# Projection tiles in four matmuls of 512 columns: tables and stores turned to that token order

## The chip, the cores and the metric

The kernel runs on one NeuronCore of a Trainium2 chip: TensorE (PE, with its weight loads shown apart as PEld), VectorE (DVE), ScalarE (ACT), GpSimd (POOL), a queue engine (SyncE, SP), and 16 DMA engines between HBM and the on-chip memory. Results of TensorE land in PSUM, eight banks of 512 float32 columns on 128 partitions. The metric is the device time of one execution in microseconds; smaller is better. Engines run their own instructions in the order in which they were issued and meet only at semaphores.

## What is computed

Attention with an exponential feature map over 8 batches, 8 heads, 576 tokens and 64 features a head; its output, 512 features a token, goes through a gated long convolution:

```python
proj = np.einsum('bhsd,df->bhsf', x, w_phi)            # phi(x), for q and for k
proj = proj - np.max(np.abs(proj), axis=-1, keepdims=True)
phi  = np.concatenate([np.exp(proj), np.exp(-proj)], axis=-1)
kv, z = einsum('bhsf,bhsd->bhfd', k_p, v), np.sum(k_p, axis=2)
x = (q_p @ kv) / (q_p . z + 1e-06)                     # then 512 features a token
x1, x2, x3 = np.split(x @ w_proj, 3, axis=-1)          # w_proj is 512 x 1536
x2_conv = np.fft.irfft(np.fft.rfft(x2, axis=1) * np.fft.rfft(filter_fft, axis=0), n=576, axis=1)
out = (x1 * x2_conv * x3) @ w_out                      # 8 x 576 x 512, float32
```

The Fourier transforms are matmuls with tables of sines that the kernel makes for itself at its start.

## The kernel before

**Tokens.** A token is 9 t + j, with t from 0 to 63 and j from 0 to 8. The 64 tokens of j = 4 go a way of their own (the steps whose names end in `t`). The other 512 stand in four blocks of 128, numbered a = 2 g + d: g is the lower or upper half of the t, d = 0 holds j = 0 to 3, and d = 1 holds j = 8 to 5, kept mirrored (t and j both falling), since the transform works on sums and differences of a token and its mirror image.

**Order of work.** A planner's word list, `PLAN` (L31 to L197), fixes the order: each word is one step with its batch, its part and its PSUM bank (`X1,3,2@4`), the steps are issued in the order of the list, and each engine and each queue works its own steps in that order. Batches overlap: the attention of one batch stands between the convolution steps of the batches before it. The steps that matter here:

- `Pq` and `ex` (L658, L686) make the feature tiles `Eq` of the queries; `NE` (L772) picks a block of `Eq` for each a and multiplies it with `KVs`; `xn` (L795) divides and writes 128 tokens by four blocks by 128 features of a pair of heads.
- `trx` (L816) turns `xn` of one pair of heads, v = 0 to 3, into `xT` by a DMA transpose on SP's queue. `trh` (L602) does the same for q and k of a later batch, `trxt` (L821) for j = 4.
- `f1`, `f2` (L845, L851) form sums and differences of the blocks of `xn`, `F` (L856) multiplies them with the table `D`, and `X2` (L893), `Y1`, `m3` and `I` (L967) carry the convolution on to the inverse table `inv`, whose columns are tokens in the order that `gi_nr` (L337) lays down.
- `X1` and `X3` call `proj` (L914): one tile is 128 output features by the 512 tokens, summed over the four kt (the v of `xT`). Each batch has four tiles of `X1` and four of `X3`, 64 tiles in all. It fills one PSUM bank with eight matmuls of 256 columns: first d = 0 for the four kt, then d = 1 for the four kt, reading the d = 1 blocks backwards, so that its tokens come out rising. Each matmul loads its 128 by 128 weights first.
- `O` (L1017) multiplies with `wout`, `Oe` (L1023) copies 128 tokens by 512 features to one of four `o` buffers, and `st` (L1026) sends each half of it, 64 rows of 2 KB, to rows j, j + 9, j + 18, ... of the output. Nine halves go out for each batch: two for each c of 0 to 3, and one for c = 4, the tokens of j = 4 of a pair of batches. c = 0 and 1 hold j = 0 to 3, c = 2 and 3 hold j = 5 to 8. 67 of the 72 stores are issued on SP's queue, and five of the last batch on ACT's.

SP's queue carries the transposes and the stores in one order. An `o` buffer is written again only when both its stores have landed.

Of the kernel before, what the change touches and what calls it, by code (L numbers as in the profile page):

```python
# [16 lines left out]
SEQ = 576  # L17
# [4 lines left out]
IOTA = dict(allow_small_or_imprecise_dtypes=True)  # L22
# [20 lines left out]
mlo,DVE,0 maxkt,0@2 trm,0@6 rve,DVE,1@0 em,m,0,0 em,m,0,1 trme,DVE,0@6 em,p,0,0 vs,POOL,m,0,0  # L43
trh,k,1,1 Pqt,0@4 exkt,p,0@2 Qn,1,0@6 Pq,0,1@0 exqt,p,0@4 maxq,1,0@6 exqt,m,0@4 fl_loadt em,p,0,1
ex,q,m,0,1@0 Qn,1,3@6 vs,DVE,p,0,0 load,k,2 Pq,0,2@4 Pq,0,3@2 ex,q,p,0,1@0 w_load,proj,2
maxq,1,3@6 vs,POOL,p,0,1 ex,q,p,0,3@2 Pk,1,1@0 maxk,1,1@0 KV,0,0@6 ex,q,m,0,3@2 ex,q,p,0,2@4
Qnt,1@2 w_load,proj,0 KVe,DVE,0,0@6 ex,q,m,0,2@4 vs,POOL,m,0,1 maxqt,1@2 NE,0,1@6 Qn,1,2@2
ex,k,p,1,1@0 rc,0,1@6 Pq,0,0@4 xn,0,1@6 ft,ACT maxq,1,2@2 trx,0,1 KV,0,1@6 load,v,1 ex,k,m,1,1@0
load,q,2 trh,k,2,0 ex,q,p,0,0@4 Pk,1,0@0 KVe,DVE,0,1@6 w_load,proj,1 maxk,1,0@0 NE,0,2@6
ex,q,m,0,0@4 zl,POOL NE,0,3@2 rc,0,2@6 Pk,1,3@4 ex,k,p,1,0@0 xn,0,2@6 rc,0,3@2 NE,0,0@6  # L50
ex,k,m,1,0@0 xn,0,3@2 rc,0,0@6 NEt,0@2 f1,POOL,0,1,1 ex,k,p,1,3@4 xn,0,0@6 Pkt,1@0 rct,0@2
# [4 lines left out]
X1,0,3@1 late He,ACT,2,0@7 maxk,1,2@4 f2,POOL,0,0,0 He,ACT,3,1@2 X1,0,2@6 He,ACT,1,1@0 mlo,DVE,1  # L56
X1,0,0@7 X1e,DVE,0,3@1 f2,POOL,0,0,1 ex,k,m,1,2@4 He,DVE,3,0@2 trm,1@3 X1e,ACT,0,0@7 trh,q,2,0
vs,DVE,m,1,0 F,0,3@4 load,v,2 trme,ACT,1@3 F,0,1@0 Fe,ACT,0,3@4 X3,0,0@2 X1e,DVE,0,2@6 em,m,1,1
vs,POOL,p,1,0 trh,k,2,1 Fe,ACT,0,1@0 F,0,2@4 tm,0,0@2 F,0,0@6 Fe,ACT,0,2@4 Pq,1,1@0 Fe,ACT,0,0@6
Pk,2,0@2 vs,POOL,m,1,1 KV,1,0@4 ex,q,p,1,1@0 maxk,2,0@2 ex,q,m,1,1@0 X2,0,3@7 KVe,DVE,1,0@4  # L60
em,p,1,1 ex,k,p,2,0@2 X3,0,2@6 vs,POOL,p,1,1 Y1,0,3@7 Xl,ACT,0 X2,0,2@1 trxt,0 ex,k,m,2,0@2
# [10 lines left out]
exqt,p,1@2 ym,POOL,0,3 trx,1,3 xn,1,2@0 NEt,1@2 KVe,ACT,2,0@4 O,0,3@6 rct,1@2 f2,DVE,1,0,0 trx,1,2  # L72
f2,DVE,1,0,1 O,0,0@7 f1,DVE,1,1,1 Oe,ACT,0,3@6 f1,DVE,1,1,0 xnt,1,1@2 Qn,2,3@4 f2,POOL,1,1,1
Qnt,2@0 xnt,1,0@2 O,0,1@6 maxq,2,3@4 O,0,2@3 Oe,ACT,0,1@6 Oe,DVE,0,0@7 F,1,0@4 f2,DVE,1,1,0
Oe,ACT,0,2@3 st,SP,0,0,1 F,1,1@6 maxqt,2@0 Fe,ACT,1,0@4 trh,q,3,1 F,1,3@2 Fe,DVE,1,1@6 F,1,2@0
Fe,ACT,1,3@2 Qn,2,2@4 Fe,ACT,1,2@0 trx,1,0 Pk,2,3@6 maxq,2,2@4 X2,1,1@3 ex,k,m,2,3@6 X2,1,2@0
trh,q,3,0 ex,k,p,2,3@6 Y1,1,1@3 X2,1,3@1 mhi,2 maxk,2,3@6 mlo,POOL,2 trh,k,4,1 load,q,4 trm,2@5
X1,1,3@2 trme,ACT,2@5 load,v,3 Y1,1,2@0 X1,1,2@4 st,SP,0,2,0 X1e,ACT,1,3@2 st,SP,0,3,1 Pq,2,1@2
Y1,1,3@1 X1e,ACT,1,2@4 Qn,3,2@6 em,m,2,1 X1,1,0@4 ex,q,p,2,1@2 maxq,3,2@6 m3,POOL,1,1 X3,1,2@5
ex,q,m,2,1@2 Pq,2,0@0 X1e,ACT,1,0@4 tm,1,2@5 Qn,3,0@6 em,p,2,1 ex,q,p,2,0@0 X3,1,0@3 vs,POOL,m,2,1  # L80
maxq,3,0@6 ex,q,m,2,0@0 NE,2,1@4 tm,1,0@3 Pq,2,2@6 Xl,ACT,1 rc,2,1@4 Pkt,3@0 X3,1,3@2 xn,2,1@4
vs,POOL,p,2,1 exkt,p,3@0 exkt,m,3@0 trx,2,1 NE,2,0@4 ex,q,p,2,2@6 tm,1,3@2 X2,1,0@3 rc,2,0@4
xn,2,0@4 trxt,1 ex,q,m,2,2@6 X1,1,1@2 Y1,1,0@3 f1,POOL,2,0,0 Pqt,2@6 trh,k,4,0 X1e,ACT,1,1@2
KV,2,1@4 maxkt,3@0 exqt,m,2@6 exqt,p,2@6 f1,DVE,2,0,1 Pk,3,1@2 st,SP,0,2,1 KVe,ACT,2,1@4 Pq,2,3@0
f2,POOL,2,0,1 maxk,3,1@2 trx,2,0 NE,2,2@6 ex,q,p,2,3@0 X2,1,4@4 m3,POOL,1,0 rc,2,2@6 ex,q,m,2,3@0
xn,2,2@6 trh,q,4,1 X1t,1@5 Y1,1,4@4 NEt,2@6 X1te,ACT,1@5 NE,2,3@0 ex,k,p,3,1@2 trx,2,2 rct,2@6
# [113 lines left out]
class Kernel:  # L200
# [136 lines left out]
    def gi_nr(self):  # L337
        g, s = self.nc.gpsimd, self.scr
        self.nr = s.tile([128, 288], FP32, name="nr")
        g.iota(self.nr[:, 0:256], pattern=[[5, 2], [1, 4], [9, 32]], base=1,  # L340
               channel_multiplier=0, **IOTA)
        g.iota(self.nr[:, 256:288], pattern=[[9, 32]], base=5, channel_multiplier=0, **IOTA)

    def ident(self):
# [409 lines left out]
    def KV(self, b, X):  # L754
        for w in range(2):
            v = 2 * X + w
            for s, g in enumerate("pm"):
                E, Ft = self.at("Ek" + g, 4 * b + v), self.at("Fk" + g, b)
                vg = self.turn_of("v" + g, (b, X))
                a = (2 * w + s) * 65  # L760
                for j in range(9):
                    for u in range(2):
                        r = slice(64 * u, 64 * u + 64)
                        e = E[r, j % 2, j // 2, :] if j < 8 else Ft[r, w, X, :]
                        self.mm(self.pb(u, a, a + 65), e, vg[r, w, j, :], start=(j == 0),  # L765
# [6 lines left out]
    def NE(self, b, v):  # L772
        KVs = self.at("KVs", b)
        for u in range(2):
            for a in range(4):
                for s, g in enumerate("pm"):
                    y = 2 * (1 - u if a % 2 else u) + a // 2
                    E = self.turn_of("Eq" + g, (b, v))[:, y, a % 2, :]
                    self.mm(self.pb(u, 65 * a, 65 * a + 65), E, KVs[:, u, v, s, :],  # L779
                            start=(s == 0), stop=(s == 1))  # L780

    def NEt(self, b):
        KVs = self.at("KVs", b)
        for X in range(2):
            for u in range(2):
                for s, g in enumerate("pm"):
                    E = self.at("Fq" + g, b)[:, 2 * X + u].rearrange("f w t -> f (w t)")
                    self.mm(self.pb(X, 130 * u, 130 * u + 130), E,
                            KVs[:, u, 2 * X:2 * X + 2, s, :], start=(s == 0), stop=(s == 1))
# [66 lines left out]
    def F(self, b, v):  # L856
        xf, xt, D, Dt = self.at("xf", b), self.at("xnt", b), self.at("D"), self.at("Dt")
        for e in range(2):
            self.mm(self.pb(e, 0, 288), xt[:, v // 2, :], Dt[:, v % 2, 288 * e:288 * e + 288],  # L859
                    start=True, stop=False)  # L860
        for e in range(2):
            for s in range(2):
                self.mm(self.pb(e, 144 * s, 144 * s + 144), xf[:, v, 2 * s + e, :],  # L863
                        D[:, 288 * e + 144 * s:288 * e + 144 * s + 144], start=False,
                        stop=(s == 1))

    def Ft(self, b, X, bank2):
        xt, Dt = self.at("xnt", b), self.at("Dt")
        for e in range(2):
            for w in range(2):  # L870
                r, bank = slice(64 * w, 64 * w + 64), bank2 if w else self.bank
                self.mm(self.ps[:, bank + e, 0:288], xt[r, X, :],
                        Dt[r, w, 288 * e:288 * e + 288], start=True, stop=False)

    def Fs(self, b, v):
        xf, D = self.at("xf", b), self.at("D")
        for e in range(2):
            for s in range(2):
                self.mm(self.pb(e, 144 * s, 144 * s + 144), xf[:, v, 2 * s + e, :],
                        D[:, 288 * e + 144 * s:288 * e + 144 * s + 144], start=False,  # L880
                        stop=(s == 1))

# [30 lines left out]

    def proj(self, b, f0, m):  # L914
        w, x = self.at("wproj"), self.at("xT", b)
        o = self.pb(0).rearrange("p (g d x) -> p d g x", g=2, d=2)
        for d in range(2):
            for kt in range(4):
                y = x[:, kt].rearrange("p (g d) x -> p d g x", g=2)
                self.mm(o[:, d], w[:, kt, f0 + 128 * m:f0 + 128 * m + 128],  # L920
                        y[:, 1, ::-1, ::-1] if d else y[:, 0], start=(kt == 0),
                        stop=(kt == 3))

    def projt(self, b, f0):
        w, x = self.at("wproj"), self.at("xTt", b)
# [47 lines left out]
                self.mm(self.pb(e, 0, 288), l, inv[:, 2 * e + i if i < 2 else 4 + e, :],  # L973
                        start=(i == 0), stop=(i == 2))

    def It(self, b, m):
        c, inv = slice(128 * m, 128 * m + 128), self.at("inv")
        for e in range(2):
            r = slice(64 * e, 64 * e + 64)
            self.mm(self.pb(e, 0, 288), self.at("T4", b)[r, c], inv[r, 4 + e, :], start=True,  # L980
                    stop=False)

    def Is(self, b, m):
        c, inv = slice(128 * m, 128 * m + 128), self.at("inv")
        for e in range(2):
            for i in range(2):
                self.mm(self.pb(e, 0, 288), self.at(f"T{2 * e}", b)[:, i, c],
                        inv[:, 2 * e + i, :], start=False, stop=(i == 1))

    def Ie(self, b, m):  # L990
        self.nc.scalar.copy(self.turn_of("es", (b, m)), self.pb(0, 0, 288))  # L991

# [32 lines left out]

    def st(self, eng, b, c, i):  # L1026
        o = self.turn_of("o", (b, c))
        bb, j = (b, (0, 2, 5, 7)[c] + i) if c < 4 else (b - 1 + i, 4)
        dict(SP=self.nc.sync, ACT=self.nc.scalar)[eng].dma_start(
            out=self.out[bb][j:SEQ:9, :], in_=o[64 * i:64 * i + 64, :])  # L1030

    def run(self):
        self.scratch = ExitStack()
# [52 lines left out]
```

## Time and profile before

| | us |
|---|---|
| median of three runs | 308.5 (307.57 to 310.66) |
| the profiled execution | 307.3 |
| its span, first to last instruction | 305.5 |

A row of a group reads: line, engine, operation, tiles out and in, shape, count, then busy time and mean time of one, then the idle time of the engine just before such instructions and what ended it. In the chain of work that ended last, each piece has its start, its length and its engine. Matmuls are pipelined: the duration of one is longer than the distance to the next, so their pace is read from a run of them in the chain. The issue of a DMA is a row of the queue's engine (SPq, ACTq); its time to landing runs from there to its last completion.

| engine | busy us | share of the span |
|---|---|---|
| TensorE | 275.5 | 90% |
| VectorE | 262.3 | 86% |
| ScalarE | 223.0 | 73% |
| GpSimd | 216.4 | 71% |

### The profile page before, as it was taken

The numbers are of one execution on the slowest core, as the hardware profiler recorded it, in microseconds if no ns is written. First come the engines' busy times: TensorE is split into PE (matmuls) and PEld (weight loads), VectorE is DVE, ScalarE is ACT, GpSimd is POOL, SyncE is SP. The second block draws the span as 40 slices with busy tenths as digits, with TensorE's granted clock in tenths as the row PEclk, the third lists the DMA queues.
The fourth block names the chain that finished last, engine by engine and source line by source line (L and its number), as shares of the span: only waits on it lengthen the run. The fifth ranks groups of instructions, "written<-read, shape, count | busy, mean of one in ns | idle before, by whom it ended". The sixth has DMA issues, their size and how long they took to land.

```text
span 305.5 us, 10146 instructions
## 1 busy us (share of the span) xinstructions
PE 275.5 (90%) x4253; PEld 199.7 (65%) x4287; DVE 262.3 (86%) x448; ACT 223.0 (73%) x360; POOL 216.4 (71%) x180
## 2 busy tenths in 40 slices
PE   8357687999989999999999999999999889999993
PEld 3235654778558876767767776777577656786751
DVE  7798799898897998799988999787997899789863
ACT  1998986888359978876987688976757988843240
POOL 8346968699528689869799998956289397970240
PEclk9855999999999999999999999999999999999998
DMA  7997999999989987997699959994063440322056
GB/s 144 242 200 133 206 136 179 157 153 191 108 118 187 144 136 134 189 177 144 131 151 154 140 92 177 165 163 102 4 139 65 103 89 10 72 55 60 2 120 190
DMA packets 72734, 40.18 MB, mean 132 GB/s; under 512 B 53040, under 2 KB 67504, under 8 KB 72688
## 3 DMA queue, kind: packets, MB, share of 16 engines
q1 hardware_dynamic: 57472, 22.62, 45.4%
q0 software_dynamic: 14816, 16.25, 35.6%
q8 instruction: 33, 0.54, 0.8%
q10 hardware_dynamic: 400, 0.66, 0.6%
q14 instruction: 13, 0.11, 0.1%
HBM read 33.75 MB, written 9.44 MB: 141 GB/s over the span
## 4 chain that ended last, share of the span: by engine, by line
PE 69%; DVE 15%; ACT 5%; DMA 5%; issue 4%; SPq 0%; DVEq 0%
PE ps L920 15%; PE ps L898 9%; PE ps L1020 8%; PE ps L973 6%; PE ps L765 5%; DMA xT<-xn 5%; PE ps L779 3%; DVE mk L708 3%; PE ps L666 3%; PE ps L929 2%; PE ps L672 2%; PE ps L639 2%; PE ps L859 2%; PE ps L318 2%; PE ps L863 2%
## 5 line engine op out<-in xcount | busy, mean ns | idle before, releaser
L920 PE MATMUL ps<-xT,wproj 128*128 128x256 bf16 x512 | 64.2, 273 | 2.3 <-DMA xT<-xn 2.2
L920 PEld LDWEIGHTS <-wproj 128*128 128x128 bf16 x512 | 48.3, 98 | 12.7 <-issue 2.9
L708 DVE TENSOR_REDUCE mk<-ps 128x8 f32<-128x1024 f32 (+1 forms) x40 | 44.2, 1109 | 6.1 <-PE ps L632 5.4
L708 DVE TENSOR_REDUCE mq<-ps 128x8 f32<-128x1024 f32 (+1 forms) x40 | 44.0, 1109 | 5.1 <-PE ps L639 3.6
L912 POOL TENSOR_TENSOR T<-T,T 128x1024 bf16<-128x1024 bf16 x15 | 31.9, 2127 | 18.3 <-DVE T L908 18.2
L1009 POOL TENSOR_TENSOR yT<-cv,x1s 128x576 bf16<-128x576 f32 x27 | 34.3, 1295 | 11.6 <-DVE cv L994 11.5
L750 POOL TENSOR_TENSOR vm<-vn,vm 128x1152 bf16<-128x1152 bf16 x15 | 32.9, 2194 | 9.3 <-ACT vm L744 9.3
L694 ACT ACTIVATE Ekp<-ps 128x1024 bf16<-128x1024 f32 x32 | 33.1, 1033 | 3.9 <-PE ps L632 2.6
L694 ACT ACTIVATE Ekm<-ps 128x1024 bf16<-128x1024 f32 x32 | 33.0, 1032 | 4.0 <-DVE mk L708 2.6
L750 POOL TENSOR_TENSOR vp<-vn,vp 128x1152 bf16<-128x1152 bf16 x15 | 32.2, 2155 | 5.1 <-ACT vp L744 5.1
L694 ACT ACTIVATE Eqp<-ps 128x1024 bf16<-128x1024 f32 x32 | 32.8, 1026 | 3.4 <-PE ps L672 3.2
L1020 PE MATMUL ps<-wout,yT 128*128 128x512 bf16 x130 | 34.0, 380 | 1.2 <-DVE yT L1009 0.4
L694 ACT ACTIVATE Eqm<-ps 128x1024 bf16<-128x1024 f32 x32 | 32.5, 1028 | 3.3 <-PE ps L672 2.5
L847 POOL TENSOR_TENSOR SD<-xn 128x512 bf16<-128x512 bf16 x23 | 26.3, 1160 | 10.1 <-DVE xn L798 8.6
L853 POOL TENSOR_TENSOR xf<-SD 128x512 bf16<-128x512 bf16 x24 | 27.8, 1169 | 7.1 <-DVE SD L847 5.7
L898 PE MATMUL ps<-wproj,XF 128*128 128x512 bf16 x116 | 30.3, 380 | 0.9 <-ACT XF L299 0.2
L973 PE MATMUL ps<-inv,T 128*128 128x288 bf16 x192 | 27.6, 286 | 0.1
L994 DVE TENSOR_TENSOR cv<-es,ps 128x288 f32<-128x288 f32 x64 | 25.6, 443 | 1.4 <-ACT es L991 1.1
L299 ACT CAST x1s<-ps 128x512 bf16<-128x512 f32 (+1 forms) x34 | 17.9, 543 | 11.8 <-PE ps L920 9.9
L961 DVE TENSOR_TENSOR x1s<-ps,x1s 128x512 bf16<-128x512 f32 x32 | 21.7, 684 | 5.0 <-PE ps L920 4.1
L991 ACT COPY es<-ps 128x288 f32<-128x288 f32 x32 | 12.9, 404 | 14.2 <-PE ps L973 13.7
L798 DVE TENSOR_TENSOR xn<-ps,r 128x512 bf16<-128x512 f32 x32 | 22.0, 689 | 0.9
(176 smaller groups left out, 657.5 us busy)
## 6 DMA issues: line engine op xcount, KB each, us to landing
out_dram<-o SPq DMA_DIRECT2D x67, 128.0 KB, 2.5
vn<-in_v_dram POOLq DMA_DIRECT2D x8, 576.0 KB, 7.2
qn<-in_q_dram POOLq DMA_DIRECT2D x7, 576.0 KB, 9.2
kn<-in_k_dram POOLq DMA_DIRECT2D x7, 576.0 KB, 9.2
wproj<-in_moe_w_proj_dram POOLq DMA_DIRECT2D x3, 512.0 KB, 8.5
fl<-in_moe_filter_fft_dram SPq DMA_DIRECT2D x8, 128.0 KB, 5.6
out_dram<-o ACTq DMA_DIRECT2D x5, 128.0 KB, 3.0
qn<-in_q_dram POOLq DMA_DIRECT2D x2, 288.0 KB, 6.5
```

The source lines that it names most:

```text
L694: self.nc.scalar.activation(e, p, AF.Exp, bias=0.0, scale=1.0 if g == "p" else -1.0)
L708: self.nc.vector.tensor_reduce(out=out, in_=src, axis=AX.X, op=ALU.max, apply_absolute_value=True)
L750: self.eng(eng).tensor_tensor(out=t[:, :, :, 0:64], in0=self.at("vn", b)[:, 2 * X:2 * X + 2], in1=t[:, :, :, 64:65].to_broadcast([128, 2, ...
L847: self.eng(eng).tensor_tensor(out=o[:, :, 2 * i:2 * i + 2, :], in0=x[:, :, 0:2, :], in1=x[:, :, 2:4, :], op=ALU.subtract if i else ALU.add)
L853: self.eng(eng).tensor_tensor(out=o[:, :, 2 * i:2 * i + 2, :], in0=x[:, :, 0:4:2, :], in1=x[:, :, 1:4:2, :], op=ALU.subtract if i else ALU ...
L898: self.mm(self.pb(0), l, w[:, kt, 512:1024], start=(kt == 0), stop=(kt == 3))
L912: self.eng(eng).tensor_tensor(out=Y, in0=Y, in1=self.at(f"T{2 * e + 1}", b), op=ALU.add)
L920: self.mm(o[:, d], w[:, kt, f0 + 128 * m:f0 + 128 * m + 128], y[:, 1, ::-1, ::-1] if d else y[:, 0], start=(kt == 0), stop=(kt == 3))
L973: self.mm(self.pb(e, 0, 288), l, inv[:, 2 * e + i if i < 2 else 4 + e, :], start=(i == 0), stop=(i == 2))
L994: self.nc.vector.tensor_tensor(out=self.turn_of("cv", (b, m))[:, :, odd, :], in0=self.turn_of("es", (b, m)).rearrange("p (x t) -> p x t", ...
L1009: self.eng(eng).tensor_tensor(out=self.at("yT", b)[:, m, 0:SEQ], in0=self.turn_of("cv", (b, m)).rearrange("p x h t -> p (x h t)"), in1=sel ...
L1020: self.mm(self.pb(0), y[:, kt, 128 * c:128 * c + 128], w[:, kt, :], start=(kt == 0), stop=(kt == 3))
```

## The change

`proj` issues four matmuls of 512 columns, one for each kt, and reads each `xT[:, kt]` straight through. The mirrored blocks are no longer read backwards, so they keep their falling order up to the output. `NE` picks the blocks of `Eq` for d = 1 in the order that fits, `F` takes the differences of d = 1 in that order, `gi_nr` writes the token numbers of the mirrored half falling (two iota of 128 columns in place of one of 256), and the stores of c = 2 and 3 (32 of the 72) go to rows whose t falls: their destination, 64 rows with one step between them before, becomes two halves h of 32 rows t each, with t walked backwards. `PLAN` is the same word for word, and so is the number of stores and of bytes. Four functions that no step called (`Ft`, `Fs`, `It`, `Is`) are taken out.

```diff
@@ gi_nr
-        g.iota(self.nr[:, 0:256], pattern=[[5, 2], [1, 4], [9, 32]], base=1,
-               channel_multiplier=0, **IOTA)
+        for d in range(2):
+            z = 1 - 2 * d
+            g.iota(self.nr[:, 128 * d:128 * d + 128], pattern=[[z, 4], [9 * z, 32]],
+                   base=288 if d else 1, channel_multiplier=0, **IOTA)
         g.iota(self.nr[:, 256:288], pattern=[[9, 32]], base=5, channel_multiplier=0, **IOTA)
@@ NE
-                for s, g in enumerate("pm"):
-                    y = 2 * (1 - u if a % 2 else u) + a // 2
-                    E = self.turn_of("Eq" + g, (b, v))[:, y, a % 2, :]
+                for s, sg in enumerate("pm"):
+                    g, d = a // 2, a % 2
+                    y = 2 * (1 - u) + 1 - g if d else 2 * u + g
+                    E = self.turn_of("Eq" + sg, (b, v))[:, y, d, :]
@@ F
-                self.mm(self.pb(e, 144 * s, 144 * s + 144), xf[:, v, 2 * s + e, :],
+                self.mm(self.pb(e, 144 * s, 144 * s + 144), xf[:, v, 2 * (1 - s) + 1 if e else 2 * s, :],
@@ proj
-        o = self.pb(0).rearrange("p (g d x) -> p d g x", g=2, d=2)
-        for d in range(2):
-            for kt in range(4):
-                y = x[:, kt].rearrange("p (g d) x -> p d g x", g=2)
-                self.mm(o[:, d], w[:, kt, f0 + 128 * m:f0 + 128 * m + 128],
-                        y[:, 1, ::-1, ::-1] if d else y[:, 0], start=(kt == 0),
-                        stop=(kt == 3))
+        for kt in range(4):
+            self.mm(self.pb(0), w[:, kt, f0 + 128 * m:f0 + 128 * m + 128],
+                    x[:, kt].rearrange("p a x -> p (a x)"), start=(kt == 0), stop=(kt == 3))
@@ st
-        bb, j = (b, (0, 2, 5, 7)[c] + i) if c < 4 else (b - 1 + i, 4)
+        bb, j = (b, (0, 2, 8, 6)[c] + (-i if c > 1 else i)) if c < 4 else (b - 1 + i, 4)
+        dst = self.out[bb][j:SEQ:9, :]
+        if c in (2, 3):
+            dst = dst.rearrange("(h t) d -> h t d", h=2)[:, ::-1, :]
         dict(SP=self.nc.sync, ACT=self.nc.scalar)[eng].dma_start(
-            out=self.out[bb][j:SEQ:9, :], in_=o[64 * i:64 * i + 64, :])
+            out=dst, in_=o[64 * i:64 * i + 64, :])
```

More of the change, by code (lines that the diff above doesn't have):

```diff
@@ L862, in F @@
             for s in range(2):
-                self.mm(self.pb(e, 144 * s, 144 * s + 144), xf[:, v, 2 * s + e, :],
[L864 to L879, printed above, removed]
+                self.mm(self.pb(e, 144 * s, 144 * s + 144), xf[:, v, 2 * (1 - s) + 1 if e else 2 * s, :],
                         D[:, 288 * e + 144 * s:288 * e + 144 * s + 144], start=False,
@@ L974, in I @@
                         start=(i == 0), stop=(i == 2))
[L976 to L988, printed above, removed]
     def Ie(self, b, m):
```

## The prediction

> **What bounds the kernel now.** The page comes first: the span, the busy shares, the chain that ended last, then the groups of the changed matmuls and the issues of the stores.
>
> ```profile
> span 305.5 us, 10146 instructions
> ...
> PE 275.5 (90%) x4253; PEld 199.7 (65%) x4287; DVE 262.3 (86%) x448; ACT 223.0 (73%) x360; POOL 216.4 (71%) x180
> ...
> q1 hardware_dynamic: 57472, 22.62, 45.4%
> ...
> q10 hardware_dynamic: 400, 0.66, 0.6%
> ...
> PE 69%; DVE 15%; ACT 5%; DMA 5%; issue 4%; SPq 0%; DVEq 0%
> ...
> L920 PE MATMUL ps<-xT,wproj 128*128 128x256 bf16 x512 | 64.2, 273 | 2.3 <-DMA xT<-xn 2.2
> L920 PEld LDWEIGHTS <-wproj 128*128 128x128 bf16 x512 | 48.3, 98 | 12.7 <-issue 2.9
> ...
> out_dram<-o SPq DMA_DIRECT2D x67, 128.0 KB, 2.5
> ```
>
> TensorE bounds the kernel: 90% busy, 69% of the chain. The DMA pieces of the chain are 5%, all of them `xT`: transposes that arrive as PE wants them. The changed matmuls are 64.2 us of busy time, so the question is first how much quicker a tile becomes. That is read from the chain in order of time (start, length, what):
>
> ```profile
> 141.25 4.13 DMA xT<-xn
> ...
> 272.91 0.58 SPq L1029
> 273.54 2.51 DMA xT<-xn
> ...
> 283.42 0.86 PE ps L898 x4
> 284.28 0.86 PE ps L1020 x4
> 285.14 2.62 PE ps L920 x24
> ```
>
> Three projection tiles back to back take 2.62 us, so 0.873 for a tile of eight; four matmuls of 512 columns, as `X2` and `O` have them, take 0.86. The matmul goes by its columns, and the 98 ns of a weight load hide behind 109 ns of matmul already. One reads here that halving the number of matmuls halves neither time nor anything on the path.
>
> **The change part by part.**
>
> *The tiles.* 64 tiles gain about 0.01 us each: 0.64 us. A second gain is at late transposes. PE's timeline:
>
> ```profile
> 144.25 0.50 PE L920 MATMUL ps<-xT,wproj 128*128 128x256 bf16 x3
> 145.42 1.58 PE L920 MATMUL ps<-xT,wproj 128*128 128x256 bf16 x13 [0.67 <-DMA xT<-xn]
> ...
> 275.73 1.29 PE L920 MATMUL ps<-xT,wproj 128*128 128x256 bf16 x8
> ```
>
> At 144.25 the tile stops after three matmuls, because kt = 3 is not there; five of 0.109 are still to do when it lands (0.55), after the change one of 0.215: 0.33 less. The tile at 275.73, which waits for kt = 1, has seven left (0.76), then three (0.65): 0.11 less. With one more stop like the first that makes about 0.8. Together -1.4 us; the ends are 0 (if all of it is eaten by waits of other engines) and -1.4. A rule says more: the Trainium skill, "TensorE: Matmul & The Clock Gate", section "Back-to-back issue gap", gives about 131 ns for each matmul of 512 columns in a sustained stream, which would make a tile 0.52 us and the gain 64 x 0.35 = 22 us. The rows above show 215 ns, which is the isolated formula of the same section (512 / 2.4 + 2.5), so I don't count with 131.
>
> *`NE`, `F`.* The same number of matmuls and loads of the same shapes, other indices: nothing to either side. *`PLAN`*: no step passes another.
>
> *`gi_nr`.* One iota of 256 columns becomes two of 128, at the start on POOL, ahead of two q and k loads on POOL's queue.
>
> ```profile
> 3.72 0.42 POOL L340 IOTA nr<- 128x256 f32 x1
> 4.06 0.19 POOL L342 IOTA nr<- 128x32 f32 x1
> ...
> 4.66 2.06 DVE L422 TENSOR_SCALAR turn<-nr,cols 128x288 f32<-128x288 f32 x5
> ```
>
> An iota of 128 lies between 0.19 (32 columns) and 0.42 (256), so the pair costs between -0.04 and 0.42 more; about 0.2. DVE reads `nr` at 4.66, 0.4 after it is done at 4.25, which covers it, and without that cover it would be 0.2. I count 0.
>
> *The stores of c = 2 and 3.* This part decides. The destination was 64 rows with one step; now it is two halves of 32 rows, with 2 as its outermost count. How is a store spread over the 16 DMA engines? The DMA view of 0 to 14 us and of 291 to 306 us (queue, packets, MB, share of 16 engines):
>
> ```profile
> q1 hardware_dynamic: 800, 1.11, 25.5%
> ...
> fl<-in_moe_filter_fft_dram SPq DMA_DIRECT2D x8, 128.0 KB, 5.6
> ...
> phi<-in_w_phi_dram SPq DMA_DIRECT2D x2, 32.0 KB, 4.3
> ```
>
> ```profile
> GB/s 0 0 0 98 224 186 197 235 131 38 218 208 208 197 180 0 60 202 224 197 104 191 322 175 246 339 290 251 355 208 322 284 224 186 16 0 0 0 0 0
> ...
> q1 hardware_dynamic: 1040, 1.70, 49.6%
> q10 hardware_dynamic: 400, 0.66, 12.1%
> ...
> out_dram<-o SPq DMA_DIRECT2D x13, 128.0 KB, 2.4
> out_dram<-o ACTq DMA_DIRECT2D x5, 128.0 KB, 3.0
> ```
>
> Five ACT stores make 400 packets, 80 each: 64 rows and 16 more, one completion for each engine. The 13 on SP do the same (1040 / 13), and the ten early loads too (800 / 10), though `fl` walks 32 by 2 rows: its outermost count is 32. So each transfer here has an outermost count that 16 divides, and goes to 16 engines in equal parts. No row shows a count of 2. The bounds are: still 16 engines (no cost), or whole outer slices to an engine, which is two engines with 32 rows each. I take two, as what is seen fits a split of the outer count and nothing in it would split an inner one. The Trainium skill says so outright: "DMA: Bandwidth & Descriptors", section "Why a DMA increments its semaphore by 16 and not by 1", has a transfer run on the largest k up to 16 that divides both sides' slowest counts, and for queues like SP's and ACT's on the lowest-numbered k. The 16 completions agree; k = 2 is in no run yet.
>
> The price of a row: q10 kept the engines busy for 12.1% of 16 x 15 us, 29 us for 320 rows, 91 ns. q1 gives 119 us for 832 rows, 143 ns, its waits included. The best slice, 355 GB/s, is 22.2 GB/s an engine, 92 ns for 2 KB. I take 92, as two of the three agree, and 143 as the upper end. A store then holds two engines for 32 rows, 2.94 us, where it held all 16 for 4 rows, 0.37: +2.58, and what stands behind it on SP's queue waits that long on those two engines; I take a transpose to use all 16, as a store does now, so that it lands late as a whole. (By the same DMA page, section "Specifications", 27 GiB/s an engine would make a row 71 ns, and the end of the kernel, next, about 6 us shorter.)
>
> *The end.* Of the 18 stores issued from 291.21 on, eight are turned (batches 6 and 7, c = 2 and 3).
>
> ```profile
> 291.21 10.43 SPq L1029 DMA_DIRECT2D out_dram<-o  x13
> ...
> DMA to landing us min/median/max: 2.2/2.6/10.5
> ```
>
> The two engines get 8 x 32 + 10 x 4 = 296 rows, 27.2 us. The first byte moves at about 293.0 (issue, plus the least landing of 2.2, less 0.37 of its own rows), so the last lands at 320.2, where now it is about 304.2 (301.2 for the last issue and 3.0 on ACT): +16.0. The engines don't run dry: batch 7's copies wait for `o` buffers, but batch 6's stores alone are 13 us of rows. The tiles' gain moves the start of this stretch, so it stays in the sum.
>
> *Before the end.* 24 more turned stores. The lower bound is 0, all hidden; the upper 24 x 2.58 = 62 us, each on the path. I count the three places where rows show little room.
> - `trx,7,1` at 273.54 lies in the chain right behind a turned store (272.91): +2.6.
> - `trh,q,7,1`: two transposes of q of batch 7 follow four stores, three of them turned.
>
> ```profile
> 222.77 2.39 SPq L1029 DMA_DIRECT2D out_dram<-o  x4
> 225.28 2.76 SPq L603 DMA_TRANSPOSE qT<-qn  x2
> ...
> DMA to landing us min/median/max: 3.3/3.3/3.3
> ...
> 230.88 0.40 PE L639 MATMUL ps<-wphi,qT 64*128 64x128 bf16 x8
> ```
>
> The first lands at 225.28 + 3.3 = 228.6, and `Qn` reads it at 230.88, 2.3 later. Three times 2.58 is 7.7, so PE stops for 5.4. Less if the queue is late in issuing anyway.
> - `trx,3,3` at 141.25, in the chain, two us behind a turned store:
>
> ```profile
> 139.28 0.55 SPq L1029 DMA_DIRECT2D out_dram<-o  x1
> 139.92 2.55 SPq L817 DMA_TRANSPOSE xT<-xn  x2
> ```
>
> +2.6, and 7.7 if the two turned stores ten us before it are still in the way. Everywhere else I count 0: what hides it is the time between a transpose's landing and its use, and 2.58 a store is the cost if that is gone.
>
> Sum: -1.4 + 16.0 + 2.6 + 5.4 + 2.6 = +25.2 on the profiled execution's 307.3 (span 305.5 and 1.8 around it), 332.5 us. That execution is 1.2 under the median of 308.5, so the change is given against either as some 8%.
>
> **The rivals.**
> - *The stores keep 16 engines* (the other side): the queue folds the two halves into 64 rows, or splits the inner count. For it: no transfer of before used fewer. Against: a falling step inside a rising one can't be one step, and nothing seen splits an inner count. Then only the tiles count: 307.3 - 1.4 = 305.9, within 1%. It decides with 16 completions to a store.
> - *Two engines, but only the end pays*: the middle has room, since DMA is 5% of the chain. Against: that 5% is just such transposes. 307.3 - 1.4 + 16.0 = 321.9.
> - *The middle pays more*: rows at 143 ns beside the loads, `o` buffers that come free late and hold up ScalarE: each 2.58 beyond the three counted, from `trx,3,3` (+5.1) on; four more make 347.9.
> - *The tiles gain what the number of matmuls suggests* (the 131 ns): 307.3 - 22 = 285; the rows of `O` and `X2` speak against it.
>
> **How the numbers follow.** Two engines, end and some of the middle: 0.50, with a range of its own from 318 to 344. Only the end: 0.18. More in the middle: 0.09. Sixteen engines: 0.20. Tiles much quicker: 0.03. About 1% is what a measurement of this kernel can tell from no change. Slower: 0.50 + 0.18 + 0.09 = 0.77; same 0.20; faster 0.03. The forecast is 332.5; as the sixteen engines hold 0.20, the range has to reach to them: 305.5 to 346.
>
> **What would show it.** Completions: with two engines, q10 has two turned stores of five, 2 x 66 + 3 x 80 = 372 packets in place of 400, and q1 30 x 14 = 420 fewer, 57052; with sixteen, 400 and 57472. The landing time of a turned store rises from 2.5 by about 2.6, and by ten or more at the end. The last store lands at 15 us or more after the last copy to `o`, and PE and DVE stand idle there. L920 has 256 matmuls of 128x512 at 380 ns, and three tiles back to back take 2.6 us as before; if they take under 2.4, I have the tiles wrong. If the packets fall and the time doesn't rise, the row price is wrong, or two engines alone run much quicker than 92 ns a row.

## The result, and the profile after

The changed kernel takes 356.0 us, the median of six runs (351.4 to 361.2), beside 309.6 for six runs of the kernel before: a ratio of 1.144, with a 95% interval of 1.134 to 1.153. Ratios and their intervals, here and below, are of the executions within 1.5% of the fastest of their kernel alone, since the others show a slower state of the chip. The prediction said slower, 332.5 us, with a range that ended at 346.0. The sign and the cause were right, the size was not: 24 us too little. The profiled execution took 351.4 us, its span 349.6, where the one of before had 305.5.

From the page of the changed kernel (span, busy time, the packets of SP's queue q1 and of ACT's queue q10, the chain that ended last, the changed matmuls):

```profile
span 349.6 us, 9667 instructions
...
PE 287.8 (82%) x4031; PEld 180.2 (52%) x4031; DVE 264.8 (76%) x448; ACT 223.5 (64%) x360; POOL 216.4 (62%) x181
...
q1 hardware_dynamic: 57052, 22.62, 49.9%
...
q10 hardware_dynamic: 372, 0.66, 0.5%
...
PE 50%; DMA 23%; DVE 12%; ACT 6%; issue 4%; SPq 3%; POOL 0%; ACTq 0%; DVEq 0%; POOLq 0%
...
L904 PE MATMUL ps<-xT,wproj 128*128 128x512 bf16 x256 | 65.2, 386 | 4.1 <-DMA xT<-xn 3.9
```

Two packet counts answer the first question: 372 and 57052 are the numbers that the prediction gave for two completions a store, 14 fewer than sixteen for each of the 32 turned stores. The bytes are the same (22.62 and 0.66 MB). TensorE's busy time is 287.8 us, 12 more, at a granted clock of 0.911 over the execution where it was 0.969; the transfers' share of the chain went from 5% to 23%. The line of the tiles has the same busy time as before (65.2 against 64.2): 256 matmuls of 386 ns for 512 of 273, both being overlapped lengths.

The end, in the chain in order of time (start, length, what):

```profile
314.53 2.59 PE ps L904 x12
...
321.15 7.32 DMA out_dram<-o
...
329.18 12.66 DMA out_dram<-o
...
341.96 0.69 DVE o L301
```

Three tiles still take 2.6 us. From 321 on the chain is stores, and copies into `o` that wait for a buffer that a store has not let go; PE ends its last matmul at 329.7, 20 us before the end. One sign that the prediction gave did not come: the span ends 7 us after the last copy to `o` (342.65), not 15 or more, since the copies themselves wait for stores. The waits, grouped (engine, line and what it waited for; us in total, times, longest):

```profile
DVE o L301 <- DMA out_dram<-o: 14.1, 3, 9.9
ACT o L299 <- DMA out_dram<-o: 7.7, 3, 3.1
...
PE ps L641 <- DMA qT<-qn: 5.4, 1, 5.4
...
PE ps L912 <- issue: 3.0, 1, 3.0
```

Where in the span did the 44 us arise? SP issues the same steps in the same order in every version, so the start of one and the same transpose in two traces shows how far one is behind the other. The base taken here is the changed kernel with straight stores (`e12_straight_again`, below; span 307.8), which differs in nothing else; it was itself 2.3 us longer than before, so 41.8 of the 44 us are looked for. SP's issues in the timeline (start, length of the issue, what), first of the changed kernel, then of the straight one:

```profile
103.02 3.65 SPq L605 DMA_TRANSPOSE kT<-kn  x1
...
152.13 1.98 SPq L605 DMA_TRANSPOSE qT<-qn  x1
...
158.62 1.17 SPq L825 DMA_TRANSPOSE xTt<-xnt  x1
...
196.17 6.40 SPq L605 DMA_TRANSPOSE kT<-kn  x1
...
204.51 7.04 SPq L605 DMA_TRANSPOSE qT<-qn  x1
...
232.80 1.37 SPq L605 DMA_TRANSPOSE kT<-kn  x1
...
245.59 9.89 SPq L605 DMA_TRANSPOSE qT<-qn  x2
...
263.63 1.20 SPq L820 DMA_TRANSPOSE xT<-xn  x1
...
301.40 2.51 SPq L825 DMA_TRANSPOSE xTt<-xnt  x1
```

```profile
102.86 1.32 SPq L605 DMA_TRANSPOSE kT<-kn  x1
...
145.04 1.35 SPq L605 DMA_TRANSPOSE qT<-qn  x1
...
148.81 1.17 SPq L825 DMA_TRANSPOSE xTt<-xnt  x1
...
186.27 1.53 SPq L605 DMA_TRANSPOSE kT<-kn  x1
...
189.99 6.71 SPq L605 DMA_TRANSPOSE qT<-qn  x1
...
211.94 1.38 SPq L605 DMA_TRANSPOSE kT<-kn  x1
...
228.35 2.74 SPq L605 DMA_TRANSPOSE qT<-qn  x2
...
239.19 1.20 SPq L820 DMA_TRANSPOSE xT<-xn  x1
...
277.09 1.20 SPq L825 DMA_TRANSPOSE xTt<-xnt  x1
```

Subtracting row from row gives the lag, and its growth from one row to the next says where the time went (us; the last line is the spans, 349.6 - 307.8 = 41.8):

| up to, in the straight kernel | lag | growth | the prediction counted there |
|---|---|---|---|
| 102.86 | 0.2 | 0.2 | 0 |
| 145.04 | 7.1 | 6.9 | 0 |
| 148.81, past `trx,3,3` | 9.8 | 2.7 | 2.6 |
| 186.27 | 9.9 | 0.1 | 0 |
| 211.94 | 20.9 | 11.0 | 0 |
| 228.35 | 17.2 | -3.6 | 0 |
| 239.19, past `trh,q,7,1` | 24.4 | 7.2 | 5.4 |
| 277.09 | 24.3 | -0.1 | 0 |
| the end, with `trx,7,1` | 41.8 | 17.5 | 18.6 |

The rows of the counted places and of the end are within 2 us of their terms. The rows that the prediction had at nothing add up to 14 us: 6.9 early, and 11.0 beside the loads, of which 3.6 came back, as a late queue can catch up. PE's own lag has no such swing. Matching its 4031 matmuls in the two traces one by one, PE is 9.8 us late ahead of that stretch (at 180 us of the straight kernel), 17.4 behind it (at 225), 24.4 behind the wait for `qT`, 26.9 behind `trx,7,1`, and the span ends 41.8 late.

One counted row came out for another reason. PE waits for no `xT` at all between 140 and 165 us of the changed kernel, so `trx,3,3` cost nothing; PE's one wait there is 2.9 us in the middle of a step `I`, on nothing that the profile names. That wait and others, of which the prediction counted only the last two, in the chain of the changed kernel (start, length, what):

```profile
101.73 7.80 DMA xTt<-xnt
...
118.83 6.00 DMA out_dram<-o
...
146.71 2.94 issue
...
203.26 17.10 DMA out_dram<-o
...
245.59 10.95 DMA qT<-qn
...
300.11 5.47 DMA xT<-xn
```

The first is `trxt,1`, which PE awaits for 2.8 us (0.7 in the straight kernel). The two stores are turned ones, and ScalarE waits for their `o` buffers (1.6 and 3.0 us).

### The profile page after: what moved, and what is told of

The parts are those of the page before. It is cut to its first block, busy times and chain, and to the rows that moved or that the text cites. A ratio compares the mean times of both kernels' runs of the same rounds, so it can differ in the third digit from the quotient of the medians.

```text
span 349.6 us, 9667 instructions
## 1 busy us (share of the span) xinstructions
PE 287.8 (82%) x4031; PEld 180.2 (52%) x4031; DVE 264.8 (76%) x448; ACT 223.5 (64%) x360; POOL 216.4 (62%) x181
## 3 DMA queue, kind: packets, MB, share of 16 engines
q1 hardware_dynamic: 57052, 22.62, 49.9%
## 4 chain that ended last, share of the span: by engine, by line
PE 50%; DMA 23%; DVE 12%; ACT 6%; issue 4%; SPq 3%; POOL 0%; ACTq 0%; DVEq 0%; POOLq 0%
DMA out_dram<-o 12%; PE ps L904 10%; PE ps L885 7%; PE ps L989 5%; PE ps L956 4%; PE ps L767 4%; PE ps L782 4%; DMA xTt<-xnt 3%; DMA qT<-qn 3%; DMA xT<-xn 3%; DVE mk L710 3%; PE ps L668 2%; PE ps L641 2%; PE ps L674 2%; PE ps L912 2%
## 5 line engine op out<-in xcount | busy, mean ns | idle before, releaser
L904 PE MATMUL ps<-xT,wproj 128*128 128x512 bf16 x256 | 65.2, 386 | 4.1 <-DMA xT<-xn 3.9
L710 DVE TENSOR_REDUCE mq<-ps 128x8 f32<-128x1024 f32 (+1 forms) x40 | 44.0, 1111 | 10.3 <-PE ps L641 9.2
L904 PEld LDWEIGHTS <-wproj 128*128 128x128 bf16 x256 | 23.7, 99 | 29.4 <-issue 6.0
L989 PE MATMUL ps<-wout,yT 128*128 128x512 bf16 x144 | 37.2, 394 | 0.4 <-DVE yT L978 0.4
L956 PE MATMUL ps<-inv,T 128*128 128x288 bf16 x192 | 29.1, 295 | 2.9 <-issue 2.9
L885 PE MATMUL ps<-wproj,XF 128*128 128x512 bf16 x128 | 31.3, 380 | 0.2 <-ACT XF L299 0.2
L960 ACT COPY es<-ps 128x288 f32<-128x288 f32 x32 | 12.8, 401 | 26.7 <-PE ps L956 26.1
L299 ACT COPY o<-ps 128x512 f32<-128x512 f32 x24 | 14.1, 600 | 16.7 <-PE ps L989 9.0
```

What stands on the lines that cost most here:

```text
L299: self.nc.scalar.copy(dst, src)
L710: self.nc.vector.tensor_reduce(out=out, in_=src, axis=AX.X, op=ALU.max, apply_absolute_value=True)
L885: self.mm(self.pb(0), l, w[:, kt, 512:1024], start=(kt == 0), stop=(kt == 3))
L904: self.mm(self.pb(0), w[:, kt, f0 + 128 * m:f0 + 128 * m + 128], x[:, kt].rearrange("p a x -> p (a x)"), start=(kt == 0), stop=(kt == 3))
L989: self.mm(self.pb(0), y[:, kt, 128 * c:128 * c + 128], w[:, kt, :], start=(kt == 0), stop=(kt == 3))
```

## The experiments

In all of them only the form of stores, their queue, or what feeds them, is changed. `A` in front of a line is the changed kernel.

**One part alone: the stores made straight, and the turned stores on the kernel before.**

```
A  e1_straight, e12_straight_again
-        if c in (2, 3):
-            dst = dst.rearrange("(h t) d -> h t d", h=2)[:, ::-1, :]

before  e3_stores_alone
+        if c in (2, 3):
+            dst = dst.rearrange("(h t) d -> h t d", h=2)[:, ::-1, :]
```

> The changed kernel, but the 32 stores of c = 2 and 3 go out with one rising step, 64 rows each (so within these blocks the rows of the output stand in falling token order). Everything else of the change stays: the tiles of 512 columns, the tables, the order of blocks. Theory A (the whole loss is the stores whose outermost count is 2, so that two DMA engines carry 32 rows each): q10 400 packets, q1 57472, the time at or just under that of before, ratio 0.99 to 1.00. Rival B (the tiles or the tables cost in the middle too; +2.4 us stood in the trace before the first turned store): ratio 1.01 to 1.05. Rival C (the tiles gain much): below 0.98.

> The kernel of before with nothing changed but the form of the stores of c = 2 and 3: two groups of 32 rows in falling order, as in the change (rows of these blocks then stand in falling order in the output). Theory A: q10 372 and q1 57052 packets, ratio 1.14 to 1.16, the change's own loss and some 1.4 us more. Rival B (part of the middle comes of the tiles or the tables): clearly less, 1.05 to 1.10.

Straight stores: ratio 1.004 (0.996 to 1.012), packets 57472 and 400. Turned stores on the old kernel: 1.161 (1.151 to 1.171), 57052 and 372. The stores hold the whole loss, within the 1% that these intervals leave; the turned stores alone cost even a little more than the change, which no run explains. Rival C falls, and B with the second run, which it had at 1.10 at most. The straight kernel was run again with more rounds, on the chip of the last group:

> The changed kernel with straight stores once more, on the same chip as the three runs before it and with more rounds: the base for the two runs with four turned stores, and what the tiles of 512 columns bring by themselves. The prediction's term for the tiles is -1.4 us, a ratio of 0.995; the run before of this kernel gave 1.004 (0.996 to 1.012). Rival (the tiles gain nothing or lose): 1.00 to 1.01.

Ratio 0.997 (0.992 to 1.002). The term of -1.4 us, 0.995, lies inside, and so does nothing at all: the two can't be told apart.

**The number of engines.** The same falling step, with other outermost counts:

```
A  e2_outer16: h=16 for h=2        e2b_outer4: h=4 for h=2
```

> The changed kernel, but a turned store writes its rows as 16 rising groups of 4 rows in falling order, in place of 2 groups of 32 (so the rows stand permuted in the output). Same bytes, same falling innermost step, outermost count 16. Theory A (the outermost count of 2 is what costs): 16 completions a store, q10 400 and q1 57472 packets, ratio 0.99 to 1.01. Rival (a falling step costs by itself, whatever the engines): ratio above 1.10 as the change has it.

> The changed kernel, but a turned store writes 4 rising groups of 16 rows in falling order. Theory A: 4 completions a store, so q10 has 2 x 68 + 3 x 80 = 376 packets and q1 30 x 12 = 360 fewer than 57472, 57112; 16 rows an engine, 1.5 us at 92 ns, in place of 32. At the end 8 x 16 + 40 / ... = 128 rows of turned stores on the four engines and 10 x 4 = 40 of straight ones, 168 x 92 ns = 15.5 us, in place of 27.2: the end some 4 us over before. Middle: between nothing and half of the 29 us. Ratio 1.01 to 1.06. Rival (the time per store is fixed, whatever the count of engines below 16): ratio as the change, 1.14.

Sixteen groups: 1.005 (0.996 to 1.013), 57472 and 400 packets. Four: 1.052 (1.042 to 1.062), 57112 and 376, the counts given ahead of the run. So a falling step costs nothing that can be told from noise, and the price goes with the rows that one engine gets: 4 rows, nothing; 16 rows, 5%; 32 rows, 14%. The rule of the Trainium skill, "DMA: Bandwidth & Descriptors", section "Why a DMA increments its semaphore by 16 and not by 1" (the engines used are the largest number up to 16 that divides both slowest counts), agrees with the counts for 16, 4 and 2.

**Where the price is paid.** Turned stores in the last two batches only, and in the others only:

```
A  e4_end_only:     if c in (2, 3) and b > 5:
A  e5_middle_only:  if c in (2, 3) and b < 6:
```

> The changed kernel with only the eight turned stores of batches 6 and 7 left on two engines; the 24 of batches 0 to 5 go out with one rising step (their rows then stand in falling order). Theory A with the sizes read from the changed kernel's trace (end +14.7 of +44.1): ratio 1.045 to 1.055, the prediction's own end of +16.0 would be 1.052. Rival (the end is dear only because the kernel came to it late and with a full queue): under 1.03.

> The other part: the 24 turned stores of batches 0 to 5 on two engines, the eight of batches 6 and 7 with one rising step. The changed kernel's transfers run +29 us late before the end, some 3 of them there in the kernels with straight stores as well. Theory A: the two parts add up, so ratio 1.085 to 1.10. The prediction counted three places in the middle, 10.6 us: 1.035. Rival (the slack before the end takes the middle's delay in): under 1.03.

The end 1.045 (1.021 to 1.070), the middle 1.092 (1.079 to 1.105); together 0.137, and the change has 0.144. The parts add up. The end agrees with its 16.0 us, which would be 1.052, though its interval is wide; the middle is nearly three times the 10.6 us that the prediction counted.

**Which stores of the middle.** SP issues four turned stores just ahead of the stretch where the lag grows by 11 us:

```
A  e9_four_straight
-        if c in (2, 3):
+        if c in (2, 3) and (b, c, i) not in ((2, 3, 0), (2, 2, 0), (3, 3, 1), (2, 2, 1)):
```

> The changed kernel with four of its 32 turned stores made straight: (2,3,0), (2,2,0), (3,3,1) and (2,2,1), which SP issues within some four us just ahead of the transposes of q of batch 6 and of x of batch 5, where the changed kernel's lag grows by some 11 us. Theory A1 (what costs is where turned stores bunch in front of transposes that are soon needed: the queue holds SP's next issues up): these four give back 8 to 12 us, ratio 1.105 to 1.12. Rival A2 (each turned store of the middle costs about the same, 29 us over 24, 1.2 us): 5 us, ratio 1.125 to 1.13.

1.113 (1.098 to 1.127), where A1 had 1.105 to 1.12 and A2 1.125 to 1.13. By the middle of the interval the four give back 3%, about 10 us; the interval alone does not exclude A2. So a pair was made, each with four turned stores and no others: at that place, and at one without loads.

```
A  e10_four_busy:   if (b, c, i) in ((2, 3, 0), (2, 2, 0), (3, 3, 1), (2, 2, 1)):
A  e11_four_quiet:  if (b, c, i) in ((4, 2, 0), (4, 3, 0), (4, 2, 1), (5, 2, 1)):
```

> The changed kernel with only four turned stores left, (2,3,0), (2,2,0), (3,3,1) and (2,2,1), the other 28 with one rising step (falling rows in those blocks). Around these four POOL issues three loads of 576 KB (v and q), and all sixteen engines are busy: three loads and eleven transfers of SP's queue in 32 us, even straight stores land after 6 us. Theory A4 (two engines lose 2.58 us of their time a turned store, whatever queue it is on, and it costs that much where loads keep those engines busy): 4 x 2.58 = 10.3 us over the kernel with straight stores, ratio about 1.035. Theory A2 (every turned store of the middle costs the same 1.2 us): 5 us, ratio 1.02. If it takes many turned stores to fill the slack: 1.00 to 1.01.

> The pair to the run before it: only four turned stores left as well, but (4,2,0), (4,3,0), (4,2,1) and (5,2,1), which SP issues in a stretch without loads, where straight stores land in 2.5 us. Theory A4 (the price is paid only where the two engines have other work that is soon needed): 0 to 2 us over straight stores, ratio 1.00 to 1.01. Theory A2 (the same for every turned store): the same 5 us as the four at the loads, 1.02.

The quiet four: 0.998 (0.993 to 1.002), nothing beside the straight kernel's 0.997, so A2's 1.02 falls. The busy four: six runs, one of 313.0 us and five of 319.6 to 324.8, each above all twelve runs of the straight kernel on that chip (306.2 to 310.6, median 308.9): 4 us more in the fastest, 11 to 16 in the others. That the four cost more here than at the quiet place is shown; how much is not, as the runs lie too far apart for a ratio with an interval. The profile is of the longest, 324.8 us, and shows where that execution lost its time. SP's issues with the busy four:

```profile
185.19 1.18 SPq L825 DMA_TRANSPOSE xTt<-xnt  x1
...
191.46 4.28 SPq L605 DMA_TRANSPOSE kT<-kn  x1
...
199.77 11.71 SPq L605 DMA_TRANSPOSE qT<-qn  x1
...
226.62 1.36 SPq L605 DMA_TRANSPOSE kT<-kn  x1
...
292.28 1.19 SPq L825 DMA_TRANSPOSE xTt<-xnt  x1
```

The row at 185.19 stands at 180.11 in the straight kernel, and no store was turned so far: PE lost these 5 us in the first 45 us, so they are not of the four stores. Against the straight kernel's rows above the lag is 5.2 at 191.46, 14.7 at 226.62 and 15.2 at 292.28: in this execution 10 us were added at the four stores, and nothing was won back. The transposes behind them take 4.28 and 11.71 us to issue, for 1.53 and 6.71. PE's lag behind the straight kernel, matmul by matmul, shows what the stretch costs in each trace (us; the last line is the spans):

| at, in the straight kernel | changed kernel | middle alone turned | four of 32 made straight | busy four | quiet four |
|---|---|---|---|---|---|
| 100 | 0.1 | 0.5 | -0.8 | 5.8 | -1.0 |
| 180, ahead of the stretch | 9.8 | 8.7 | 7.8 | 5.1 | -1.2 |
| 225, behind it | 17.4 | 19.8 | 7.1 | 15.2 | -1.4 |
| 240, past `trh,q,7,1` | 24.4 | 26.7 | 16.0 | 15.2 | -1.4 |
| 285, past `trx,7,1` | 26.9 | 29.2 | 20.2 | 15.2 | -1.4 |
| the end | 41.8 | 29.3 | 36.0 | 15.2 | -1.4 |

With the four turned the stretch costs 7.6, 11.1 and 10.1 us, and without them nothing, also where the stores around them are turned (some 2 us of that are lost again at `trh,q,7,1`). A2 had 5 us for the four, so its even price falls here too.

How the two places differ, by the straight kernel's DMA view (packets, MB and share of 16 engines of the loads' queue; then KB of one transfer and median us to landing), for 180 to 212 us and for 226 to 252 us:

```profile
q0 software_dynamic: 1584, 1.77, 48.5%
...
out_dram<-o SPq DMA_DIRECT2D x11, 128.0 KB, 5.7
vn<-in_v_dram POOLq DMA_DIRECT2D x2, 576.0 KB, 8.2
qn<-in_q_dram POOLq DMA_DIRECT2D x1, 576.0 KB, 13.9
```

```profile
out_dram<-o SPq DMA_DIRECT2D x13, 128.0 KB, 2.5
```

Beside the loads a straight store lands in 5.7 us, without them in 2.5. This is a sign of whether two engines have time to spare. That the place decides is shown; that the loads are what makes it dear is read from these rows, and no run moved them.

**Another queue.** The stretch could be dear because SP's own queue holds its transposes behind the stores:

```
A  e8_act_queue
-        dict(SP=self.nc.sync, ACT=self.nc.scalar)[eng].dma_start(
+        dict(SP=self.nc.sync, ACT=self.nc.scalar)["ACT" if c in (2, 3) else eng].dma_start(
```

> The changed kernel with all 32 turned stores issued by ACT in place of SP (two were already), at the same places of the order; two engines a store as before, so 2 x 32 rows each. q1 55072 packets, q10 2352. Theory A1 (the middle is paid because SP's own queue holds its transposes up): SP's transposes issue in 1 to 3 us again, and the middle comes down to what ACT loses by issuing 30 stores and waiting where its queue is full: ratio 1.05 to 1.09, the end's 15 us in it. Rival A3 (two engines short of time are late for every queue alike): as the change, 1.13 to 1.15. If ACT is held up in its issues for microseconds, its copies and exponentials are late, and the run decides less.

Four runs of 351.0 to 363.8 us beside 310.3 to 317.7, too far apart for an interval; the fastest over the fastest is 1.131. With the turned stores gone from its queue SP is held up as before (in an execution of 358.5 us):

```profile
204.48 3.39 SPq L605 DMA_TRANSPOSE kT<-kn  x1
207.92 11.68 SPq L605 DMA_TRANSPOSE qT<-qn  x1
```

A1 had 1.09 at most, and even the fastest run is over it: SP's queue shared with the turned stores is not what costs. A3, that whatever needs the two engines is late, is not refuted. (ACT issued 30 stores more here, which may have cost something of its own.)

**The turning moved elsewhere.** To keep the tiles of 512 columns and the reference's order, `ym` can write `yT` turned, in three pieces:

```
A  e7_turned_product (stores straight)
-        self.eng(eng).tensor_tensor(
-            out=self.at("yT", b)[:, m, 0:SEQ],
...
+        for s, d in ((slice(0, 4), 1), (slice(4, 8), -1), (slice(8, 9), 1)):
+            self.eng(eng).tensor_tensor(out=y[:, s, :, ::d], in0=cv[:, s], in1=x[:, s], op=ALU.mult)
```

> The changed kernel with the turning of the rows moved from the stores to the product ym, which writes yT: in three pieces (x = 0 to 3, x = 4 to 7 with the 32 tokens of a row written from the last to the first, x = 8), so that all stores have one rising step and the output stands in the reference's order. 64 instructions more, 54 of them on POOL (71% busy, mostly not in the chain), 0.1 to 0.3 us each by the smallest POOL operations of the trace (0.22 to 0.25 us): 6 to 16 us of POOL's time, little of it in the chain. All theories have the stores on 16 engines: q10 400, q1 57472. Ratio 1.00 to 1.02; over 1.03 if POOL's products come into the chain or a falling write is slow there.

1.015 (1.009 to 1.021), and 0.018 more than the straight stores. The product in the groups of instructions, in three pieces and (straight kernel) in one:

```profile
L982 POOL TENSOR_TENSOR yT<-cv,x1s 128x256 bf16<-128x256 f32 (+1 forms) x81 | 42.0, 551 | 9.4 <-DVE cv L963 9.3
```

```profile
L978 POOL TENSOR_TENSOR yT<-cv,x1s 128x576 bf16<-128x576 f32 x27 | 34.3, 1291 | 11.5 <-DVE cv L963 11.1
```

The pieces take 7.7 us more of POOL; the kernel loses about 5. It mends nearly all of the change's loss and is still a little slower than the kernel before. No version is faster than that one by more than the noise.

## Why the prediction was right and wrong

- *The tiles, -1.4*: three tiles take 2.59 us for 2.62, and the straight kernel's 0.997 bears out that there is next to nothing in them. The rival of 285 us fell.
- *The tables, other indices and `gi_nr` at 0*: borne out by the same run.
- *Two engines a turned store*: shown by the packets, and by the runs with 16 and 4 groups.
- *The end, +16.0*: from the first store's issue the prediction gave 29.0 us to the last landing (291.2 to 320.2). In the changed kernel the span ends 29.0 us after that issue (320.57 to 349.6), and PE's lag before it leaves 14.9 of the 41.8 us for the end. With the end alone turned the kernel loses 14 us (0.045 of 312, its base), with an interval of 6 to 22.
- *92 ns a row*: two engines at 92 ns pass 21.7 rows a us. In the run of the quiet four, three turned stores in a row pass 14 to 25 in each us from 233 to 237; straight ones reach 109 at that place. The profile has no landing time for a turned store, which the prediction wanted to see rise by 2.6.
- *`trh,q,7,1`, +5.4, and `trx,7,1`, +2.6*: right, mechanism included. The transpose of q lands after 10.95 us, where 3.3 and three stores of 2.58 make 11.0, and PE waits 5.4 for it; `trx,7,1` lands after 5.47 in place of 2.51, and PE falls 2.5 further behind.
- *`trx,3,3`, +2.6*: luck. The row shows 2.7, but PE did not wait for this transpose; it stood for 2.9 us on an instruction that waits for nothing in the profile (last section).
- *"Everywhere else I count 0"*: this is the step that failed. The middle costs 29 us by the run that turns it alone (0.092 of 312), where 10.6 were counted. In the changed kernel's trace PE is 17.4 us late before the first of the waits that came as forecast: 9.8 by 180 us, 7.6 beside the loads. The prediction had looked for transposes that PE waits for, or that have 2.3 us to spare; it overlooked `trxt,1` (2.8 us), the `o` buffers that ScalarE waits for, and PE's stops. And it had not asked how busy the two engines are where the turned stores land. With three loads of 576 KB in the engines, a straight store there already took 5.7 us, and four turned stores add 4 x 2.58 = 10.3 us to the two engines' work; at the quiet place the same four cost nothing. The rival *the middle pays more* named rows slow beside the loads, and the `o` buffers, but got 0.09 of the chance and four stores' worth of time; its 347.9 was below every run of the changed kernel too.
- *The range* ended at 346.0 although the bound of the middle was written down as 62 us. A bound that wide, with the estimate a sixth of it, had to push the range up.

What stays open is how the two engines' lost time becomes PE's in the middle. It is not one wait: beside the loads the changed kernel stands for 3.0 us at `X1t`, runs at a lower clock afterwards, and ScalarE then waits 3.0 for an `o` buffer, while the run with the busy four stands for 9.15 us in one piece (last section). The stretch costs 7.6 to 11.1 us in three traces, and 10.3 lies among them, but the fastest run with the busy four was only 4 us over the straight kernel: that each store costs its 2.58 us there is not shown. Nor did a run take apart the 9.8 us that PE is late by 180 us.

## What to carry to other kernels

Check a transfer's outermost count against the completions in the packet count: with 2, 4 and 16 it was here the number of engines that carry the transfer. A destination turned into two halves moves the same bytes on two engines out of sixteen. Price such a transfer by the engine time it adds, and let the range reach to the whole of it wherever the profile shows those engines busy (straight transfers landing in 5.7 us in place of 2.5), also where nothing in the chain waits for it yet; where they have time to spare it was free. Look behind it not only for transposes but for every buffer that it frees. A new order of tokens is best paid for where it is cheapest: in the stores it cost 44 us here, in a product before them about 5.

## What the runs showed that was not expected

PE stopped in the middle of a tile, on matmuls that wait for nothing. The fourth of the sixteen matmuls of a tile of `X1t`, batch 4, in PE's timeline, of the straight kernel and with the busy four:

```profile
199.26 0.25 PE L912 MATMUL ps<-xTt,wproj 128*128 128x64 bf16 x3
201.68 0.54 PE L912 MATMUL ps<-xTt,wproj 128*128 128x64 bf16 x13 [2.17 <-issue]
```

```profile
205.53 0.25 PE L912 MATMUL ps<-xTt,wproj 128*128 128x64 bf16 x3
214.93 0.85 PE L912 MATMUL ps<-xTt,wproj 128*128 128x64 bf16 x13 [9.15 <-issue]
```

It is the same instruction in each trace, and the stop differs: 2.2 us, 3.0 in the changed kernel, 9.2 with the busy four, 9.5 with the middle alone turned. Counting PE's matmuls and weight loads in the order of the trace, it is number 5566. The 2.9 us at 146.71 in the changed kernel stand before number 3774, which is 7 x 256 earlier. In the old kernel with turned stores, number 5566 is a matmul of another step (L765); PE stops there too, for 2.3 us, and for 8.8 us at number 5822, 256 further on. So it is the place in the instruction stream that matters and not the step.

The instruction queue q8 moves packets of 16 KB through the DMA engines, 33 in the kernel before and 31 in the changed one, some 260 matmuls and weight loads for each packet. One starts within 1.5 us of each of the stops above but the 2.3 us of the old kernel: it takes 0.96 us in the straight kernel, 2.91 with the busy four, and 8.78 at the stop of 8.8 us. The Trainium skill, "Runtime: NRT & Kernel Launch", section "Instruction fetch mechanics", says that each engine's sequencer fetches its instructions in blocks of 16 KiB by a DMA queue of its own, and that this is mostly hidden. The traces agree on the blocks, and the stops fit a fetch that comes late because the DMA engines are loaded. That is inferred: no row ties a stop to its packet, the stop of 9.15 us goes on for 7 us after its packet has ended, and the changed kernel, with more turned stores than the busy four, stands for only 3.0.

Behind the longer stops the granted clock is lower. The windows of the changed kernel around the 3.0 us (stretch, length, then busy us and instructions of PE, PEld, DVE, ACT and POOL, granted clock, DMA share, GB/s):

```profile
206.00:213.00 7.00, 4.15 (x117) 3.38 (x110) 4.12 (x9) 4.27 (x5) 3.49 (x3) 0.95 1.39 89
213.00:220.00 7.00, 6.79 (x57) 3.64 (x56) 2.04 (x4) 1.46 (x3) 2.01 (x2) 0.56 1.56 72
```

Behind each of PE's stops of 2.8, 2.9, 3.0 and 5.4 us in the changed kernel the clock is 0.50 for 3.4 to 6.8 us; behind the 2.2 us of the straight kernel it stays at 1.00. With the busy four, the thirteen matmuls behind the stop take 0.85 us in place of 0.54.
